# Linear attention and two MLPs in float32: w3 and w_out folded in plain float32, weights converted in pairs, the attention's diagonal by TensorE

## The chip, the cores and the metric

One core of one Trainium2 chip runs the whole kernel in one launch. The metric is device time in microseconds, the median of several executions. PE is the matmul engine (TensorE), DVE is VectorE, ACT is ScalarE, POOL is GpSimd, and SP is the engine whose queue issues the DMAs.

## The reference

```python
# r, k, v, w: (4, 8, 768, 48); u: (8, 48)
for t in range(S):
    cur = einsum('bhd,bhe->bhde', u[None] * kt, vt)
    y[:, :, t] = einsum('bhd,bhde->bhe', rt, state + cur)
    state = wt[:, :, :, None] * state + einsum('bhd,bhe->bhde', kt, vt)
x = y.transpose(0, 2, 1, 3).reshape(3072, 384)
x = (((x @ w1) * (x @ w2)) @ w3) @ w_out        # w1, w2 384x1024, w3 1024x1024, w_out 1024x384
h = x @ w_in                                     # 384x2048
return (h - tanh(h)) @ w_out2                    # 2048x384
```

r, k, v, w and u are float32. The weights of the two MLPs are 64-bit floats, which the kernel receives as pairs of 32-bit words and turns into float32 itself.

## The kernel before

**Weights.** `conv` (L123) loads a block of 64-bit words by a DMA on SP's queue into tile st (four buffers of 384 columns), and makes the float32 bits in tile cm: ScalarE takes the absolute value with a scale (L130), VectorE a minimum (L131), ScalarE the three low bits (L135, or VectorE in L138 and L139 for the second MLP), VectorE shifts and joins them (L136) and puts the sign in (L140). ScalarE then copies a rounded first half (fp32r, L142) and GpSimd subtracts it for the second half (L143). A product of two such tensors is `three`: three fp32r matmuls, first by second, first by first, second by first half (L155 to L157).

**Fold.** w3 @ w_out has no activation between, so the kernel multiplies them once into a 1024 x 384 matrix W. WJ cuts its eight row blocks into groups of 2, 3 and 3; each group runs over the eight blocks m of the inner dimension, converts a piece of w3 (`fold`, L305), and sums in PSUM; `fold_end` (L315) splits the sums into halves. w_out is converted along the first group.

**Attention.** The 768 steps of each batch are cut into chunks of 128; 24 chunks in all. `prep(n)` (L184) loads one, scans the decays (L207, L214), inverts block ends (R, L210 and L211), scales k and r, and sums r, u and k over a head for the diagonal cd (L218 to L221). `att(n)` (L224) multiplies k by r (psA), copies, masks by GpSimd (L242) and sets the diagonal (from chunk PED = 5 on by VectorE, L247; before that by a scaled v and an identity matmul, L287), updates the state Sb (psk, psu, L262 to L271), and sums state and masked products into psy, which becomes block n // 4 of the first MLP's input. PSUM has five banks for `big` tiles (psa, psb, acc, psW, some psh) and three for `att` tiles.

**Blocks.** The 3072 tokens are six blocks of 512. `moe1` makes for each of eight f the products psa and psb (`phase1`, L333), their product g on VectorE, and, LA1 = 2 steps later, the product with W into acc (`phase2`). Along each block the four chunks of the next block's attention are issued. w1 and w2 are converted before and during block 0; 4 of the 32 pieces of the second MLP's weights in blocks 1 to 4, 16 in block 5 and the rest in the first block of `moe2`, which runs the second MLP over six blocks.

The order of the code is the priority of the work; a planner with a table of costs puts each engine's instructions in order ahead of time, and each engine then runs its list strictly in that order. All DMAs of the kernel stand in SP's one queue. A slower path behind a flag (L544 on) is not taken with these inputs.

Of the kernel before, what the change touches and what calls it, by code (L numbers as in the profile page):

```python
# [19 lines left out]
NP = H // 2  # L20
# [54 lines left out]
def body(ctx: ExitStack, tc, rT, kT, wP, wS, vN, rN, kN, vT, u, uP, w1, w2, w3T, wo, win, wo2, out):  # L75
# [6 lines left out]
    wtp = pool("wt", 28)  # L82
# [17 lines left out]
    ub = const.tile([128, DM], F32, name="ub")  # L100
# [22 lines left out]
    def conv(src, dst, n, by_act=True):  # L123
        st = cvp.tile([128, n, 2], I32, tag="st", name="st", bufs=4)
        nc.sync.dma_start(st.rearrange("p a b -> p (a b)"), src.bitcast(I32))
        lw, hw = st[:, :, 0], st[:, :, 1]
        lb = st.rearrange("p a b -> p (a b)").bitcast(U8)[:, 3::8]
# [17 lines left out]
    def wtile(name):
        return wtp.tile([128, 2, 384], F32R, tag="wt", name=name)

    def conv_w(src, name, p=None, by_act=True):
        t = p.tile([128, 2, 384], F32R, tag="wt2", name=name) if p else wtile(name)
        conv(src, t, 384, by_act)  # L150
        return t
# [13 lines left out]
    Sb = [a1.tile([128, NP, 128], F32, name=f"Sb{i}") for i in range(2)]  # L165
# [18 lines left out]
    def prep(n):  # L184
# [5 lines left out]
        r_n = a1.tile([128, DM], F32, tag="rn", name="rn")  # L190
        k_n = a1.tile([128, DM], F32, tag="kn", name="kn")
# [5 lines left out]
        nc.sync.dma_start(r_n, rN[n])  # L197
        if n == 0:
            nc.sync.dma_start(ub, u.to_broadcast([128, DM]))
        nc.sync.dma_start(k_n, kN[n])  # L200
# [9 lines left out]
        nc.vector.tensor_scalar(out=R, in0=P[:, :, SB::SB], scalar1=1e-25, scalar2=None, op0=ALU.max)  # L210
# [4 lines left out]
        (nc.vector if n < KD else nc.gpsimd).tensor_mul(fl(k_d), fl(k_d), sx)  # L215
        nc.gpsimd.tensor_mul(r_d, r_d, P[:, :, 0:C])

        nc.gpsimd.tensor_mul(r_n, r_n, ub)  # L218
        nc.gpsimd.tensor_mul(r_n, r_n, k_n)
        cd = a2.tile([128, H], F32, tag="cd", name="cd")  # L220
        nc.vector.tensor_reduce(out=cd, in_=r_n.rearrange("p (h d) -> p h d", d=D), op=ALU.add, axis=AX.X)  # L221
        preps[n] = r_d, k_d, P, v_n, cd

    def att(n):  # L224
# [27 lines left out]
        if c < NC - 1:  # L252
# [6 lines left out]
            for h in range(H):  # L259
                p, q = divmod(h, 2)  # L260
                o = 64 * q
                nc.tensor.matmul(pu[o : o + D, p, :], ks[:, p, o : o + D], v_n[:, h, :D], start=True, stop=True)  # L262
            for q in range(2):
                o = 64 * q
                dst = Sn[o : o + D, :, o : o + D]
                pt = P[o : o + D, :, C : C + 1].to_broadcast([D, NP, D])
                if c == 0:
                    nc.vector.tensor_mul(dst, pu[o : o + D], pt)
                else:
                    nc.vector.tensor_add(dst, pu[o : o + D], So[o : o + D, :, o : o + D])  # L270
                    nc.gpsimd.tensor_mul(dst, dst, pt)  # L271
# [5 lines left out]
        for p in range(NP if c else 0):  # L277
            nc.tensor.matmul(py[:, p, :], So[:112, p, :], r_d[:112, p, :], start=(p == 0), stop=False, skip_group_check=True)
# [24 lines left out]
    w1t, w2t, Wt = [None] * NF, [None] * NF, [None] * NF  # L303

    def fold(acc, m, j, wot):  # L305
        n = WJ[j + 1] - WJ[j]
        t = gp.tile([128, 2, 384], F32R, tag="g", name="w3")
        conv(w3T[m][:, WJ[j] * 128 : WJ[j + 1] * 128], t[:, :, : n * 128], n * 128)
        for i in range(n):
            three(  # L310
                acc[i][:, :DM], lambda h: t[:, h, i * 128 : (i + 1) * 128], lambda h: wot[m][:, h, :],
                m == 0, m == NF - 1,
            )

    def fold_end(acc, j):  # L315
        for i, a in enumerate(acc):
            w = wtile("W")
            nc.scalar.copy(w[:, 0, :], a[:, :DM])
            nc.vector.tensor_sub(w[:, 1, :], a[:, :DM], w[:, 0, :].bitcast(F32))
            Wt[WJ[j] + i] = w  # L320

    def fold_acc(j):
        return [big.tile([128, TB], F32, tag="big", name="psW") for _ in range(WJ[j + 1] - WJ[j])]

# [342 lines left out]
```

## Time and profile before

| | |
|---|---|
| median of 3 runs | 952.38 us (950.01 to 952.45) |
| profiled execution | 952.03 us, span 950.1 us, granted PE clock 0.962 |
| busy in the span | PE 877.3 us, DVE 703.6, ACT 497.6, POOL 290.2 |
| chain that ended last | PE 61%, DVE 22%, issue 6%, DMA 5%, POOL 3% |

The span reaches from the first to the last instruction. Busy time is the union of an engine's instructions; matmuls are pipelined, so a record's length is not its cost: the distance between two starts is. An idle time is shown with what ended it.

### The profile page before, as it was taken

Reading aid. Unit: us, or ns where it says so; the run is one execution under the profiler, and the core shown is the slowest. Engines: PE = TensorE matmul, PEld = TensorE weight load, DVE = VectorE, ACT = ScalarE, POOL = GpSimd, SP = SyncE. Lnnn points to the kernel's source line nnn. Section 1 sums busy time; section 2 is a strip of 40 time slices with the busy share of each in tenths; the row PEclk is TensorE's granted clock in tenths of the full one; section 3 lists DMA queues with packets and bytes.
Section 4 is the critical chain, followed back from the end, with each engine's and each line's share of the span. In section 5 each row is a group of like instructions: output and inputs, shape, how many; then the busy total and the mean of one; then the engine's idle time right before and its main releaser. Section 6 shows DMA issues by size and latency. Waiting matters only on the chain.

```text
span 950.1 us, 13117 instructions
## 1 busy us (share of the span) xinstructions
PE 877.3 (92%) x4626; PEld 710.2 (75%) x4626; DVE 703.6 (74%) x1101; ACT 497.6 (52%) x927; POOL 290.2 (31%) x283
## 2 busy tenths in 40 slices
PE   3678969889999999998999989999999999999997
PEld 2467657667778777776887768888888888888885
DVE  7999999986656657656369998677676666676764
ACT  5565656533333323333245676566676576665663
POOL 5786756534434334334124512010010010000000
PEclk9777979999999999997999999999999999999999
DMA  8656745454344234333025420020020010200001
GB/s 290 200 195 188 240 156 174 142 164 136 117 115 140 95 97 152 113 94 93 1 69 186 145 78 22 1 67 1 1 67 0 26 42 1 67 1 1 34 1 37
DMA packets 45434, 89.00 MB, mean 94 GB/s; under 512 B 5424, under 2 KB 11696, under 8 KB 45360
## 3 DMA queue, kind: packets, MB, share of 16 engines
q1 hardware_dynamic: 45360, 88.09, 29.9%
q8 instruction: 38, 0.62, 0.3%
q14 instruction: 36, 0.29, 0.1%
HBM read 76.27 MB, written 9.44 MB: 90 GB/s over the span
## 4 chain that ended last, share of the span: by engine, by line
PE 61%; DVE 22%; issue 6%; DMA 5%; POOL 3%; ACT 2%; SPq 0%; DVEq 0%; POOLq 0%; ACTq 0%
PE acc L157 9%; PE acc L155 9%; PE acc L156 9%; PE psh L155 7%; PE psh L156 7%; PE psh L157 7%; DVE cm L140 3%; DVE cm L131 3%; DVE cm L136 2%; DVE P L207 2%; PE psb L155 2%; PE psa L155 2%; DVE A L247 2%; PE psb L157 2%; PE psb L156 2%
## 5 line engine op out<-in xcount | busy, mean ns | idle before, releaser
L155 PE MATMUL psh<-xt,w 128*128 128x512 f32 x288 | 112.5, 391 | 0.5 <-DVE g L331 0.5
L156 PE MATMUL psh<-xt,w 128*128 128x512 f32 x288 | 112.3, 390 | 0.0
L157 PE MATMUL psh<-xt,w 128*128 128x512 f32 x288 | 112.2, 390 | 0.0
L156 PE MATMUL acc<-g,w 128*128 128x512 f32 x288 | 112.0, 389 | 0.0
L157 PE MATMUL acc<-g,w 128*128 128x512 f32 x288 | 111.9, 389 | 0.0
L155 PE MATMUL acc<-g,w 128*128 128x512 f32 x288 | 111.3, 389 | 0.0
L143 POOL TENSOR_TENSOR w<-cm,w 128x384 fp32r<-128x384 f32 (+1 forms) x72 | 81.5, 1138 | 87.0 <-ACT w L142 85.1
L327 POOL TENSOR_TENSOR xt<-x2l,xt 128x512 fp32r<-128x512 f32 x18 | 24.0, 1350 | 249.2 <-ACT xt L326 247.5
L390 DVE TENSOR_TENSOR psh<-psh,z 128x512 f32<-128x512 f32 (+1 forms) x99 | 67.4, 681 | 42.8 <-ACT z L387 42.0
L331 DVE TENSOR_TENSOR g<-psh,g 128x512 fp32r<-128x512 f32 (+1 forms) x99 | 66.5, 672 | 42.4 <-ACT g L330 41.9
L387 ACT ACTIVATE z<-psh 128x512 f32<-128x512 f32 (+1 forms) x99 | 57.9, 584 | 71.3 <-PE psh L157 69.7
L330 ACT CAST g<-psh 128x512 fp32r<-128x512 f32 (+1 forms) x99 | 56.7, 574 | 57.4 <-DVE psh L392 56.0
L330 ACT CAST g<-psb 128x512 fp32r<-128x512 f32 x48 | 28.0, 586 | 95.1 <-DVE psb L344 95.0
L155 PE MATMUL psb<-xt,w 128*128 128x512 f32 x144 | 61.5, 427 | 16.4 <-DVE g L331 9.2
L392 DVE SCALAR_TENSOR_TENSOR psh<-s,psh 128x512 f32<-128x512 f32 (+1 forms) x99 | 67.1, 678 | 8.7
L391 DVE SCALAR_TENSOR_TENSOR psh<-s,psh 128x512 f32<-128x512 f32 (+1 forms) x99 | 67.1, 678 | 8.5 <-ACT s L388 0.5
L388 ACT ACTIVATE s<-z,qa 128x512 f32<-128x512 f32 (+1 forms) x99 | 70.5, 712 | 2.7
L389 ACT ACTIVATE s<-z,qa 128x512 f32<-128x512 f32 (+1 forms) x99 | 68.9, 695 | 0.0
L142 ACT CAST w<-cm 128x384 fp32r<-128x384 f32 (+1 forms) x72 | 36.0, 502 | 56.4 <-DVE cm L140 52.4
L155 PEld LDWEIGHTS psh<-xt,w 128*128 128x128 f32 x288 | 54.3, 188 | 12.9 <-DVE g L331 1.6
L156 PEld LDWEIGHTS psh<-xt,w 128*128 128x128 f32 x288 | 54.2, 188 | 11.2
L157 PEld LDWEIGHTS psh<-xt,w 128*128 128x128 f32 x288 | 54.2, 188 | 11.2
(112 smaller groups left out, 2126.0 us busy)
## 6 DMA issues: line engine op xcount, KB each, us to landing
st<-wo SPq DMA_DIRECT2D x24, 384.0 KB, 3.2
P<-wP SPq DMA_DIRECT2D x24, 258.0 KB, 3.5
ws<-wS SPq DMA_DIRECT2D x24, 256.0 KB, 2.9
kd<-kT SPq DMA_DIRECT2D x24, 256.0 KB, 3.2
rd<-rT SPq DMA_DIRECT2D x24, 256.0 KB, 3.3
vn<-vN SPq DMA_DIRECT2D x24, 256.0 KB, 3.6
st<-w3T SPq DMA_DIRECT2D x16, 384.0 KB, 4.1
st<-w SPq DMA_DIRECT2D x16, 384.0 KB, 3.3
```

Source lines behind the costliest of these rows:

```text
L143: nc.gpsimd.tensor_sub(dst[:, 1, :], t, dst[:, 0, :].bitcast(F32))
L155: nc.tensor.matmul(ps, lhs(0), rhs(1), start=start, stop=False)
L156: nc.tensor.matmul(ps, lhs(0), rhs(0), start=False, stop=False)
L157: nc.tensor.matmul(ps, lhs(1), rhs(0), start=False, stop=stop)
L330: nc.scalar.copy(t[:, 0, :], x)
L331: nc.vector.tensor_sub(t[:, 1, :], x, t[:, 0, :].bitcast(F32))
L387: nc.scalar.activation(out=z, in_=p, func=AF.Square)
L388: nc.scalar.activation(out=s1, in_=z, func=AF.Square, scale=QS, bias=qa[:, 0:1])
L389: nc.scalar.activation(out=s2, in_=z, func=AF.Square, scale=QS, bias=qa[:, 1:2])
L390: nc.vector.tensor_mul(p, p, z)
L391: nc.vector.scalar_tensor_tensor(out=p, in0=s1, scalar=QB1, in1=p, op0=ALU.add, op1=ALU.mult)
L392: nc.vector.scalar_tensor_tensor(out=p, in0=s2, scalar=QB2, in1=p, op0=ALU.add, op1=ALU.mult)
```

## The change

w3 and w_out are converted to float32 and multiplied as they are, one plain float32 matmul in place of three on halves. A conversion (`words`, for `conv`) covers up to 768 columns, and weights lie in pairs in memory: w1 with w2, w_in with w_out2, two blocks of w_out; tile st has two buffers. The halves of w1 and w2 are subtracted by VectorE, those of the second MLP's weights by GpSimd; all low bits go by ScalarE. Fold runs in groups of five and three, the first ahead of block 0, the second in its first three steps (LATE), with a lag of 3 there. Attention chunks are issued at steps 1, 3, 5, 7 of the first group, each with the next one's prep. The diagonal cd comes from r times k (`rk`) and four matmuls with u (psd), copied by ScalarE. R is computed by GpSimd. k and r are scaled by VectorE for the first KD = 4 chunks and by GpSimd after, rk likewise. The state tile has 64 columns for two heads' 48 in separate row halves, so its update is one instruction where there were two, and its product with r eight matmuls of 48 rows where there were four of 112.

```diff
-WJ = 0, 2, 5, 8
-FIRST = 5, 8, 10, 11
-CONV = 3
-EARLY = 20, 20, 22
-KD = 6
+WJ = 0, 5, 8
+SLOTS = 14
+FIRST = 1, 3, 5, 7
+CONV = 2
+LATE = 3, 3, 2
+KD = 4
...
+    def words(src, n, dst=None):
+        st = cvp.tile([128, n, 2], I32, tag="st", name="st", bufs=2)
+        nc.sync.dma_start(fl(st), src.bitcast(I32))
...
+        to = m if dst is None else dst.bitcast(I32)
+        nc.vector.scalar_tensor_tensor(out=to, in0=hw, scalar=SIGN, in1=m, op0=ALU.bitwise_and, op1=ALU.bitwise_or)
+        return to.bitcast(F32)
...
+    def halves_of(src, name, vec=True):
+        t = wtile(name)
+        x = words(src, 2 * DM)
+        nc.scalar.copy(t[:, 0, :], x)
+        (nc.vector if vec else nc.gpsimd).tensor_sub(t[:, 1, :], x, t[:, 0, :].bitcast(F32))
...
-        nc.sync.dma_start(r_n, rN[n])
-        nc.sync.dma_start(k_n, kN[n])
...
-        nc.vector.tensor_scalar(out=R, in0=P[:, :, SB::SB], scalar1=1e-25, scalar2=None, op0=ALU.max)
+        nc.gpsimd.tensor_scalar(out=R, in0=P[:, :, SB::SB], scalar1=3e38, scalar2=1e-25, op0=ALU.min, op1=ALU.max)
...
-        (nc.vector if n < KD else nc.gpsimd).tensor_mul(fl(k_d), fl(k_d), sx)
-        nc.gpsimd.tensor_mul(r_d, r_d, P[:, :, 0:C])
-        nc.gpsimd.tensor_mul(r_n, r_n, ub)
-        nc.gpsimd.tensor_mul(r_n, r_n, k_n)
+        by = nc.vector if n < KD else nc.gpsimd
+        rk = a1.tile([128, NP, C], F32, tag="rk", name="rk")
+        by.tensor_mul(rk, r_d, k_d)
+        by.tensor_mul(fl(k_d), fl(k_d), sx)
+        by.tensor_mul(r_d, r_d, P[:, :, 0:C])
+        pd = attp.tile([128, NP, 2], F32, tag="att", name="psd")
+        for p in range(NP):
+            nc.tensor.matmul(pd[:, p, :], rk[:, p, :], ub[:, p, :], start=True, stop=True)
-        nc.vector.tensor_reduce(out=cd, in_=r_n.rearrange("p (h d) -> p h d", d=D), op=ALU.add, axis=AX.X)
+        nc.scalar.copy(cd, fl(pd))
...
-            nc.tensor.matmul(py[:, p, :], So[:112, p, :], r_d[:112, p, :], start=(p == 0), stop=False, skip_group_check=True)
+            for q in range(2):
+                o = 64 * q
+                nc.tensor.matmul(
+                    py[o : o + 64, p, :], So[o : o + D, p, :], r_d[o : o + D, p, :],
...
-            three(
-                acc[i][:, :DM], lambda h: t[:, h, i * 128 : (i + 1) * 128], lambda h: wot[m][:, h, :],
+            nc.tensor.matmul(acc[i][:, :DM], t[:, i * 128 : (i + 1) * 128], wot[m], start=m == 0, stop=m == NF - 1)
...
+            for f in range(NF):
+                if f < len(LATE):
+                    extra[f].append(lambda ms=range(at, at + LATE[f]): fold_late(ms))
+                    at += LATE[f]
...
-        if 0 < blk < NB - 1:
+        if 0 < blk <= SLOTS - NF - NF // 2:
             extra[4].append(conv2)
...
-                extra[f] += [lambda f=f: conv2(wp2 if f < 4 else None), conv2]
+                extra[f] += [conv2] * (2 if f < 2 else 1)
-        moe1(xtile(blk), blk, extra)
+        moe1(xtile(blk), blk, extra, lag=3 if blk == 0 else LA1)
```

## Rows read from the trace of the kernel before

**Rows 1.** Busy us of PE, PEld, DVE, ACT, POOL by stretch; granted clock; DMA.

```profile
0.00:205.00 205.00, 152.46 (x932) 122.05 (x933) 193.14 (x295) 116.45 (x247) 129.91 (x128) 0.88 0.63 196
205.00:495.00 290.00, 283.34 (x1770) 225.55 (x1769) 177.28 (x269) 99.56 (x202) 109.85 (x114) 0.98 0.35 105
495.00:575.00 80.00, 73.00 (x302) 58.08 (x301) 79.69 (x149) 49.84 (x94) 31.94 (x27) 0.96 0.41 129
575.00:950.00 375.00, 368.48 (x1627) 304.47 (x1625) 253.48 (x391) 231.79 (x385) 18.46 (x15) 0.99 0.07 22
```

**Rows 2.** Timeline of PE: start us, us, line, out<-in, shapes, records.

```profile
109.42 0.34 PE L156 MATMUL psW<-wo,w 128*128 128x384 f32 x1
109.59 0.39 PE L155 MATMUL psa<-xt,w 128*128 128x512 f32 x1
...
204.69 0.50 PE L155 MATMUL psa<-xt,w 128*128 128x512 f32 x1
```

**Rows 3.** Busy time of instructions on tile cm alone (VectorE, ScalarE, GpSimd).

```profile
0.00:205.00 205.00, 120.42 (x172) 53.44 (x107) 60.94 (x52) 0.88 0.63 196
```

**Rows 4.** Groups by line, VectorE, 0:205: busy us, mean ns | idle before.

```profile
L140 DVE SCALAR_TENSOR_TENSOR cm<-st,cm 128x384 int32<-128x384 int32 x47 | 39.6, 844 | 0.5
...
L214 DVE TENSOR_TENSOR_SCAN ws<-ws,ends 128x512 f32<-128x512 f32 x9 | 13.7, 1526 | 0.1
...
L210 DVE TENSOR_SCALAR R<-P 128x64 f32<-128x64 f32 x9 | 8.3, 925 | 0.1
...
L221 DVE TENSOR_REDUCE cd<-rn 128x8 f32<-128x384 f32 x10 | 5.4, 541 | 0.0
```

**Rows 5.** Timeline of VectorE, 124.6 to 127.2 us.

```profile
124.64 1.21 DVE L214 TENSOR_TENSOR_SCAN ws<-ws,ends 128x512 f32<-128x512 f32 x1
125.76 0.53 DVE L140 SCALAR_TENSOR_TENSOR cm<-st,cm 128x384 int32<-128x384 int32 x1
126.21 0.68 DVE L215 TENSOR_TENSOR kd<-kd,ws 128x512 f32<-128x512 f32 x1
126.81 0.35 DVE L131 TENSOR_SCALAR cm<-cm 128x384 f32<-128x384 f32 x1
```

**Rows 6.** Groups by line, VectorE, 900 to 950 us.

```profile
L391 DVE SCALAR_TENSOR_TENSOR psh<-s,psh 128x512 f32<-128x512 f32 x6 | 4.2, 696 | 0.6
...
L391 DVE SCALAR_TENSOR_TENSOR psh<-s,psh 128x256 f32<-128x256 f32 x6 | 2.6, 429 | 0.6
```

**Rows 7.** Groups by line, GpSimd (POOL), 0 to 205 us.

```profile
L143 POOL TENSOR_TENSOR w<-cm,w 128x384 fp32r<-128x384 f32 x36 | 42.4, 1180 | 24.5 <-ACT w L142 24.4
...
L242 POOL TENSOR_SCALAR_AFFINE_SELECT A<-A 128x512 f32<-128x512 f32 x17 | 13.4, 805 | 6.0 <-ACT A L240 6.0
```

**Rows 8.** Timeline of PE, one attention chunk at full clock.

```profile
297.88 0.56 PE L262 MATMUL psu<-vn,ks 128*48 128x48 f32 x16
298.38 1.16 PE L278 MATMUL psy<-rd,Sb 112*128 112x128 f32 x8
299.47 1.09 PE L281 MATMUL psy<-A,vn 128*64 128x128 f32 x16
...
300.93 1.93 PE L236 MATMUL psA<-rd,kd 48*128 48x128 f32 x16
302.78 0.50 PE L155 MATMUL psa<-xt,w 128*128 128x512 f32 x1
303.12 0.39 PE L156 MATMUL psa<-xt,w 128*128 128x512 f32 x1
303.35 0.40 PE L157 MATMUL psa<-xt,w 128*128 128x512 f32 x1
```

**Rows 9.** Waits of PE, 495 to 575 us: us, times, longest.

```profile
PE psb L155 <- DVE g L331: 4.0, 2, 2.1
```

**Rows 10.** Waits of SP's queue, 0 to 205 us: us, times, longest.

```profile
SPq L125 <- DVE cm L140: 93.0, 46, 6.6
```

**Rows 11.** DMA issues on the page: KB each, median us to landing.

```profile
st<-w3T SPq DMA_DIRECT2D x16, 384.0 KB, 4.1
```

More of the change, by code (lines that the diff above doesn't have):

```diff
@@ L74, in body @@
 @with_exitstack
-def body(ctx: ExitStack, tc, rT, kT, wP, wS, vN, rN, kN, vT, u, uP, w1, w2, w3T, wo, win, wo2, out):
+def body(ctx: ExitStack, tc, rT, kT, wP, wS, vN, vT, uB, uP, w12, w3T, wo, w45, out):
     nc = tc.nc
@@ L163, in body @@
     a2 = apool("a2", 2)
-    Sb = [a1.tile([128, NP, 128], F32, name=f"Sb{i}") for i in range(2)]
+    Sb = [a1.tile([128, NP, 64], F32, name=f"Sb{i}") for i in range(2)]
     for i in range(2):
@@ L261, in att @@
                 o = 64 * q
[L262 to L271, printed above, removed]
+                nc.tensor.matmul(pu[o : o + 64, p, :], ks[:, p, o : o + 64], v_n[:, h, :D], start=True, stop=True)
+            dst = Sn[:, :, :D]
+            pt = P[:, :, C : C + 1].to_broadcast([128, NP, D])
+            if c == 0:
+                nc.vector.tensor_mul(dst, pu, pt)
+            else:
+                nc.vector.tensor_add(dst, pu, So[:, :, :D])
+                nc.gpsimd.tensor_mul(dst, dst, pt)
         if n < PED:
@@ L451, in body, with conv2, fold_late @@
     per = TB // C
-    wot = []
     def conv1(f):
-        w1t[f] = conv_w(w1[f], f"w1_{f}")
-        w2t[f] = conv_w(w2[f], f"w2_{f}")
-    at = 0
-    for j in range(len(WJ) - 1):
-        acc = fold_acc(j)
-        for m in range(NF):
-            if j == 0:
-                wot.append(conv_w(wo[m], f"wo{m}"))
-            fold(acc, m, j, wot)
-            for n in range(per):
-                if FIRST[n] == at:
-                    att(n)
-            for f in range(CONV):
-                if EARLY[f] == at:
-                    conv1(f)
-            at += 1
-        fold_end(acc, j)
-    second = [(t, w, f) for f in range(NF2) for t, w in ((wint, win), (wo2t, wo2))][::-1]
-    def conv2(p=None):
-        if second:
-            t, w, f = second.pop()
-            t[f] = conv_w(w[f], f"w{f}", p, False)
-            if t is wint:
-                nc.vector.tensor_reduce(
-                    out=wm[:, :, f : f + 1], in_=t[f][:, 0, :].bitcast(F32).rearrange("p (a b) -> p a b", b=128),
-                    op=ALU.max, axis=AX.X, apply_absolute_value=True,
-                )
-    prep(per)
+        w12t[f] = halves_of(w12[f], f"w12_{f}")
+    second = list(range(NF2))[::-1]
+    def conv2(bound=True):
+        if not second:
+            return
+        f = second.pop()
+        w45t[f] = halves_of(w45[f], f"w45_{f}", False)
+        if bound:
+            nc.vector.tensor_reduce(
+                out=wm[:, :, f : f + 1], in_=w45t[f][:, 0, :DM].bitcast(F32).rearrange("p (a b) -> p a b", b=128),
+                op=ALU.max, axis=AX.X, apply_absolute_value=True,
+            )
+    prep(0)
+    acc = fold_acc(0)
+    for m in range(NF):
+        if m % 2 == 0:
+            conv_wo(m)
+        fold(acc, m, 0, wot)
+        for n in range(per):
+            if FIRST[n] == m:
+                att(n)
+                prep(n + 1)
+        if m >= NF - CONV:
+            conv1(m - NF + CONV)
+    fold_end(acc, 0)
+    late = []
+    def fold_late(ms):
+        if not late:
+            late.extend(fold_acc(1))
+        for m in ms:
+            fold(late, m, 1, wot)
+        if ms[-1] == NF - 1:
+            fold_end(late, 1)
     nxt = []
@@ L589, in body @@
                                 nc.sync.dma_start(xg[64 * q + D : 64 * q + 64, j, b, :], yo[a : a + 16])
-        wot = [conv_w(wo[m], "wo") for m in range(NF)]
+        wot.clear()
+        wo4.clear()
+        for m in range(0, NF, 2):
+            conv_wo(m)
         for j in range(len(WJ) - 1):
@@ L601, in body @@
                 drain(0)
+            spare.extend(sw.tile([128, 2, 2 * DM], F32R, name=f"spare{i}") for i in range(NF2 - SLOTS))
+            second.extend(range(NF2)[::-1])
             for f in range(NF2):
-                wint[f] = conv_w(win[f], "win", wp2 if f < 4 else None)
-                wo2t[f] = conv_w(wo2[f], "wo2")
+                conv2(False)
             with tc.For_i(0, NB, 1) as blk:
```

99 lines of the change are left out of this document (46 added, 53 removed).

## The prediction

> **What bounds the kernel now.** I read the busy time by stretch first, because the mean over the span hides three regimes [rows 1]. Up to 205 us VectorE is busy 193.1 of 205.0 us and PE 152.5, at a granted clock of 0.88. From 205 to 495 us PE is busy 283.3 of 290. From 495 to 575 us VectorE is busy 79.7 of 80 us again and PE 73.0. From 575 us PE is busy 368.5 of 375 with VectorE at two thirds. The timeline of PE then dates the first regime: block 0 of moe1 starts its first matmul (psa) at 109.59 us, block 1 at 204.69 us [rows 2]. So the start of block 1 is the number to forecast, then what PE has to do after it, then the second VectorE stretch.
>
> What fills VectorE up to 205 us is conversion: instructions on tile cm hold it for 120.4 us [rows 3], and they are dearer than they need be: L140 at 384 columns takes 844 ns on average, and 0.53 us in a quiet moment; the scan L214 1526 ns against 1.21 us [rows 4, 5]. What runs beside them is GpSimd, 129.9 us up to 205 us, of which the subtractions L143 on w alone are 42.4 [rows 1, 7].
>
> **The change, part by part.** The sum is made against the profiled execution, 952.03 us with a span of 950.1; the median of the three runs, 952.38, is 0.04% above it.
>
> *VectorE up to the start of block 1.* A one-pass instruction takes 0.429 us at 256 columns and 0.696 at 512 [rows 6], so 0.16 us and 1.04 ns a column: 0.56, 0.83, 0.96 us at 384, 640, 768. L131 at 0.35 us for 384 [rows 5] I take as 0.16 us and half that slope: 0.49 and 0.55 us at 640 and 768. A call of words has one L131 and two one-pass instructions: 1.47, 2.15, 2.47 us. Up to block 1 there are 8 calls of 640 columns (fold in a group of five), 8 of 384 (group of three), 4 pairs of w_out and 8 pairs of w1 and w2 at 768: 17.2 + 11.8 + 29.6 = 58.6 us. The 8 subtractions of w1 and w2, now VectorE's, add 7.7. Neighbours overlap by some 0.05 us of 0.6 at their ends [rows 5], so about 0.92 of the 66.3 shows as busy: 61 us.
> By the same rates the 172 old instructions on cm would hold VectorE for 74 us; they hold it for 120.4, so 46 us are lost beside 129.9 us of GpSimd. GpSimd now loses the halves of w3, w_out, w1, w2 and the products with rn; it keeps the selects (13.4 us [rows 7]), the v and state products (half as many of the latter), gets R nine times (64 columns, taken as under the 0.8 us of a 512-column select) and three products for each of chunks 4 to 8, 15 x 1.2 us: 50 us or so. Scaled with it the conversions lose 18 us.
> The rest of VectorE was 193.1 - 120.4 = 72.7 us. R goes (8.3 us) and so does the reduction L221 (5.4 [rows 4]), six more products of 0.68 us come (rk, kd and rd for four chunks, 12 for 6), the state update becomes one instruction for two (some 2 us), and about 6 us of its contention go by the same scale: 55. Sum 61 + 18 + 55 = 134, and 140 with the 6 us before the first bytes have been worked on.
>
> The Trainium skill's page SBUF — State Buffer, section Who interferes with whom, calls the pair of ports that VectorE shares with GpSimd an exclusive lock: the later instruction blocks for the whole of the other. By that wording every microsecond of GpSimd could cost VectorE one; on cm the trace has 46 for 130. At one for one the new VectorE time would be 61 + 55 + 50 + 6 = 172 us, more than the PE sum below, and the forecast 2 us later.
>
> *PE up to the start of block 1.* Fold was 192 matmuls of 384 columns at 0.17 us [rows 2], 33 us. A plain float32 matmul appears as two records (16 for psA's 8 matmuls): 1.85 us for 16 records of 128 columns, 0.116 each, against 0.23 us for 512 columns of fp32r [rows 8]. No row has 384 plain columns. If columns set the 0.116, a matmul takes 2 x 3 x 0.116 = 0.69 us; if the weight load does, as little as two fp32r passes, 0.34. I take 0.65, near the first, since psu's 16 records of 48 columns take 0.50 us, so that time does follow columns: 64 x 0.65 = 41.6 us, bounds 22 and 44. Attention of eight chunks by rows 8: psu, psy's two parts and psA are 0.50 + 1.09 + 1.09 + 1.85, psk's four records 0.4: 4.9 us each, and 0.9 (another set like L281, in its shadow) for five of them: 43.7 us. The new psd has 8 records with 128 x 128 weights and 2 columns; there the weights set the time, which I put at psA's 0.116 a record, and a change between plain and fp32r costs 0.1 us (the first psa after psA takes 0.34 us, the next 0.23 [rows 8]): 1.0 us a chunk, 8 us. Block 0 up to block 1, 189 matmuls of 0.226: 42.7. Sum 136 us at full clock, 154 at the old stretch's 0.88, 164 with the 10 us before the first matmul. So PE would be the longer queue, with VectorE not far off, and two such queues don't mesh fully: VectorE alone at 193 ended at 205. I take 170 us in place of 204.7: **minus 35 us**. Floor: 146 (PE at full clock), minus 59. Ceiling: 195, by the staging of rival B, minus 10.
>
> *Blocks 1 to 4.* PE is the bound, so what VectorE or GpSimd saves there counts nothing; what is added to PE counts: psd 16 x 1.0 us, and the state update's 64 weight columns for 48, some 0.1 us x 13. The read of the state by 48-row halves has 16 records for 8; the halves sit in different rows and columns of the array, and psy's column halves already go two at a time (16 records in 1.09 us, as long as 8 full ones [rows 8]): 0, bounds 0 and +1.0 us a chunk. **Plus 17 us.** Least: PE idles 6.7 us in this stretch, which can swallow some, plus 9; most, with the halves one by one, plus 33.
>
> *Block 5.* VectorE, busy 79.7 of 80 us, gets 10 paired calls of three instructions for 20 single ones of four: 25 us, and contention, for some 45. ScalarE takes over the low bits, 10 passes of 768 columns, at most about 1 us each (VectorE's 0.96 the nearest), where it is busy 49.8 of 80 [rows 1]. VectorE falls to some 60 of 80, and the 7.0 us of PE idling (the longest waits are for g [rows 9]) mostly go: **minus 6 us**, bounds 0 and minus 10. In moe2's first block 4 paired calls replace up to 12 single ones under a full PE: 0.
>
> The loads of rN and kN go; those of weights carry the same bytes in half as many issues. Sum: 952 - 35 + 17 - 6 = **928 us**.
>
> **Rivals.**
> A, the first part meshes fully: block 1 starts at 146 us, 904 us in all. For it: the chain to a fold matmul loses its last two links, copy and subtract. Against: it needs PE at full clock, and the old stretch had 0.88.
> B, the staging ring holds. There were four buffers of 384 columns; now there are two of up to 768, and SP already waits 93 us for L140 to free them [rows 10]. A buffer is held for its landing (4.1 us at 384 KB for w3T [rows 11], so perhaps 5 at 768 KB) and for two ScalarE and three VectorE passes (5 us or more). At a hold of 10 to 13 us, half of it per call, 12 calls of 768 columns and 16 shorter ones worth 10.7 take 113 to 148 us, under 170. It decides from a hold of 15 us; at 17 block 1 starts at 195 and the time is 953. Behind the held st on SP's queue stand the loads of the next preparation.
> C, slower: psd waits in PE's queue. Its rk comes from VectorE for four chunks, then from GpSimd, where it stands among products of 1.2 us and selects of 0.8; all block matmuls are queued behind psd, and it takes one of three att banks until ScalarE has copied it. With w us in each of chunks 8 to 23 the time is 928 + 16 w: a loss from 1.5 us, 968 at 2.5. Against: rk needs two loads and no scan, so it can be ready early.
> D, the float32 fold at a low clock. At 0.72 in place of 0.88, PE's 136 us are 189, block 1 starts at 199 us, and the time is 957. Against: PE is used more densely than before.
>
> **How the numbers follow.** Forecast (912 to 945) 0.66, A 0.12, B 0.09, C 0.07, D 0.06. The time is the forecast's, 928. Half of A lies below 905; most of C and half of B and D lie above 949: 0.2 is left out by 905 to 949. A difference under 0.3%, 3 us, can't be told from none here. Slower are C but for a short wait (0.06), two thirds of D (0.04) and a quarter of B (0.02): 0.12. No change takes a third of B and the rest of C: 0.04. Faster: 0.84.
>
> **What would show it.** Right: psa of block 0 near 80 us and of block 1 near 170; L131 and L140 near their quiet lengths; fold matmuls 0.65 us apart at full clock; psd 1 us a chunk; no PE gaps in block 5; moe2 as before. Wrong: SP waiting for st with VectorE idle (B), PE waiting for rk or cd (C), a clock under 0.8 up to block 1 (D), fold matmuls at 0.35 us, or any engine busier in block 5 than before.

## The result, and the profile after

The changed kernel takes 958.76 us (median; 954.84 to 966.62) beside 952.87 us for the kernel before on the same chips (950.01 to 955.07): a ratio of 1.006, 95% interval 1.0037 to 1.0083. It is slower, by 0.6%, where 928 us were forecast. The profiled execution took 959.94 us, with a span of 958.2, 8.1 us longer than before.

Busy time by stretch of the changed kernel, columns as in [rows 1]:

```profile
0.00:205.00 205.00, 165.09 (x993) 122.06 (x994) 147.26 (x211) 105.47 (x181) 60.17 (x63) 0.87 0.58 184
205.00:495.00 290.00, 285.12 (x1942) 227.35 (x1942) 161.93 (x207) 94.66 (x204) 102.41 (x103) 1.00 0.26 78
495.00:575.00 80.00, 75.57 (x320) 61.67 (x319) 66.62 (x94) 53.20 (x78) 31.14 (x17) 0.96 0.37 120
575.00:950.00 375.00, 375.00 (x1657) 310.22 (x1656) 257.65 (x396) 237.19 (x393) 19.17 (x15) 1.00 0.07 22
```

Up to 205 us VectorE fell from 193.1 to 147.3 us and GpSimd from 129.9 to 60.2: the work left them as forecast, and VectorE now idles 58 us there. But the timeline of PE shows what became of that:

```profile
97.32 0.77 PE L156 MATMUL psa<-xt,w 128*128 128x512 f32 x1 [6.60 <-DMA xt<-y]
...
199.21 0.76 PE L156 MATMUL psa<-xt,w 128*128 128x512 f32 x1 [3.92 <-DMA xt<-y]
...
500.87 0.39 PE L156 MATMUL psa<-xt,w 128*128 128x512 f32 x1
```

Block 1 starts at 199.2 us; before it was 204.7 [rows 2], and 170 was forecast. Block 5 starts at 500.9; before, its first psa was at

```profile
488.37 0.39 PE L155 MATMUL psa<-xt,w 128*128 128x512 f32 x1
```

So the span divides into: block 1's start 5.5 us earlier (forecast 35), blocks 1 to 4 301.7 us in place of 283.7, plus 18.0 (forecast plus 17), block 5 up to moe2's second block 113.8 in place of 118.0, minus 4.2 (forecast minus 6). Together plus 8.3, and the span says plus 8.1. One term of three was wrong, by 30 us. Of these, 17 had been lost before block 0, which starts at 97.3 us where "near 80" was forecast.

The waits of PE up to 205 us in the changed kernel (us in all, times, longest) give its idle time there, 39.8 us:

```profile
PE psa L156 <- DMA xt<-y: 10.5, 2, 6.6
PE psd L220 <- DVE rk L215: 8.6, 1, 8.6
PE psu L263 <- ACT ks L258: 4.9, 2, 2.8
PE psW L313 <- DVE cm L138: 4.7, 1, 4.7
PE psk L256 <- DVE y L299: 4.1, 1, 4.1
PE psb L156 <- DVE g L343: 3.1, 2, 1.9
PE psA L237 <- DVE y L299: 2.7, 1, 2.7
```

The second row is the start, 8.6 us; the other 31.2 are spread over many waits, for VectorE, ScalarE and the DMAs, none above 10.5. No single late producer is seen, so the cause had to be found by taking things away.

What did change in kind is ScalarE's waiting for weights. Its waits up to 205 us, first the kernel before, then the changed one:

```profile
ACT cl L135 <- DMA st<-w: 6.9, 5, 2.2
...
ACT cm L130 <- DMA st<-wo: 3.6, 2, 1.8
...
ACT cl L135 <- DMA st<-w3T: 2.7, 3, 1.4
```

```profile
ACT cm L131 <- DMA st<-w: 18.1, 8, 5.0
ACT cm L131 <- DMA st<-w3T: 13.9, 10, 4.2
...
ACT cl L135 <- DMA st<-w: 11.2, 5, 4.5
ACT cm L131 <- DMA st<-wo: 7.7, 4, 3.3
...
ACT cl L135 <- DMA st<-w3T: 3.2, 2, 1.7
```

From 14.1 us (with a fourth row of 0.9) to 54.1. In ScalarE's list the copies of ks, A, cd and y stand behind these waits. SP waits for the staging buffers about as long as before (93.0 us in [rows 10]):

```profile
SPq L127 <- DVE cm L138: 76.2, 27, 12.4
```

The last step to block 0 can be followed in the chain of waits (start, us):

```profile
89.56 0.30 DVE y L299
...
89.88 0.74 SPq L304
...
91.93 5.25 DMA xt<-y
...
97.32 0.77 PE psa L156
```

### The profile page after: what moved, and what is told of

Read it like the earlier page. It is cut to its first block, busy times and chain, and to the rows that moved or that the text cites. A ratio compares the mean times of both kernels' runs of the same rounds, so it can differ in the third digit from the quotient of the medians.

```text
span 958.2 us, 13061 instructions
## 1 busy us (share of the span) xinstructions
PE 902.6 (94%) x4914; PEld 722.5 (75%) x4914; DVE 634.8 (66%) x907; ACT 491.1 (51%) x855; POOL 212.9 (22%) x197
## 4 chain that ended last, share of the span: by engine, by line
PE 62%; DVE 14%; DMA 11%; ACT 5%; issue 5%; POOL 2%; SPq 1%; ACTq 0%; DVEq 0%; POOLq 0%
PE acc L157 9%; PE acc L156 9%; PE acc L158 9%; PE psh L156 7%; PE psh L157 7%; PE psh L158 7%; DMA st<-w 4%; DMA P<-wP 2%; DVE cm L138 2%; DVE P L204 2%; DMA st<-w3T 2%; DVE cm L136 2%; PE psa L156 2%; PE psb L156 2%; PE psa L158 2%
## 5 line engine op out<-in xcount | busy, mean ns | idle before, releaser
L157 PE MATMUL acc<-g,w 128*128 128x512 f32 x252 | 98.0, 389 | 0.0
L156 PE MATMUL psh<-xt,w 128*128 128x512 f32 x252 | 98.0, 389 | 0.0
L157 PE MATMUL psh<-xt,w 128*128 128x512 f32 x252 | 98.0, 389 | 0.0
L158 PE MATMUL acc<-g,w 128*128 128x512 f32 x252 | 97.9, 389 | 0.0
L158 PE MATMUL psh<-xt,w 128*128 128x512 f32 x252 | 97.9, 389 | 0.0
L156 PE MATMUL acc<-g,w 128*128 128x512 f32 x252 | 97.3, 389 | 0.0
L156 PE MATMUL psa<-xt,w 128*128 128x512 f32 x144 | 60.4, 419 | 10.5 <-DMA xt<-y 10.5
L156 PE MATMUL psb<-xt,w 128*128 128x512 f32 x144 | 60.3, 418 | 7.7 <-DVE g L343 3.8
L204 DVE TENSOR_TENSOR_SCAN P<-P,e 128x516 f32<-128x516 f32 x24 | 33.4, 1392 | 49.0 <-ACT d L200 35.4
L131 ACT ACTIVATE cm<-st 128x768 f32<-128x768 f32 (+2 forms) x44 | 36.2, 826 | 50.8 <-DMA st<-w 19.3
L356 DVE TENSOR_TENSOR psb<-psb,a 128x512 f32<-128x512 f32 x48 | 33.1, 689 | 41.7 <-PE psb L158 35.4
L158 PE MATMUL psb<-xt,w 128*128 128x512 f32 x144 | 58.5, 406 | 0.0
```

The lines of the kernel that those rows point to most:

```text
L156: nc.tensor.matmul(ps, lhs(0), rhs(1), start=start, stop=False)
L157: nc.tensor.matmul(ps, lhs(0), rhs(0), start=False, stop=False)
L158: nc.tensor.matmul(ps, lhs(1), rhs(0), start=False, stop=stop)
L204: nc.vector.tensor_tensor_scan(out=fl(P), data0=fl(P), data1=fl(e0), initial=0.0, op0=ALU.mult, op1=ALU.add)
```

## The experiments

Each is compared with the kernel before by the ratio of their times (95% interval in brackets); the kernel before, run beside each, had medians of 952.9 to 954.6 us. All starts are from the timeline of PE of one profiled execution, and "PE work" is block 1's start less all of PE's idle time ahead of it. Executions of one kernel spread by up to 12 us, so a few us between two starts can be chance. Nor has PE always done the same by block 1's start: of block 0's matmuls with W, 0.23 us each, 54 are done in the changed kernel, 57 in the kernel before, 58 in e17, 61 in e14, 63 in e3, e5 and e10. Edits are to the changed kernel, for e8 to the kernel before; lines left out are marked by "...".

| kernel | median us | ratio | block 0 | block 1 | block 5 | idle, PE work up to block 1 |
|---|---|---|---|---|---|---|
| before | 952.87 | 1 | 109.6 | 204.7 | 488.4 | 52.3, 152.4 |
| after | 958.76 | 1.006 [1.0037, 1.0083] | 97.3 | 199.2 | 500.9 | 39.8, 159.5 |
| e1 three buffers | 949.04 | 0.993 [0.9902, 0.9958] | 92.6 | 188.4 | 489.2 | 31.0, 157.5 |
| e11 two, cl in place | 960.71 | 1.0072 [1.0047, 1.0098] | 96.0 | 196.1 | 497.8 | 34.5, 161.5 |
| e4 pieces of 384 | 957.21 | 1.0038 [1.0019, 1.0056] | 96.5 | 188.4 | 489.1 | 31.7, 156.7 |
| e2 xt by ScalarE's queue | 951.03 | 0.9979 [0.9951, 1.0008] | 96.8 | 197.5 | 488.4 | 30.7, 166.8 |
| e3 no psd | 942.54 | 0.9876 [0.9839, 0.9912] | 106.8 | 198.5 | 484.0 | 45.4, 153.1 |
| e5 e1 and e3 | 933.03 | 0.9785 [0.9749, 0.9821] | 101.9 | 194.4 | 476.3 | 42.3, 152.1 |
| e6 e5 and e2 | 934.84 | 0.9791 [0.9749, 0.9833] | 100.6 | 196.7 | 476.0 | 46.2, 150.5 |
| e7 e1, e2, three ws | 939.56 | 0.9852 [0.9809, 0.9894] | 95.4 | 187.1 | 481.7 | 33.4, 153.7 |
| e8 plain fold alone | 941.27 | 0.9863 [0.9825, 0.9901] | 93.3 | 189.8 | 476.8 | 40.5, 149.3 |
| e10 e3, six of 384 | 949.57 | 0.9951 [0.9933, 0.997] | 100.4 | 198.4 | 490.1 | 46.9, 151.5 |
| e9 loads out | 942.5 | 0.9899 [0.9842, 0.9957] | 97.0 | 183.5 | 483.4 | 29.5, 154.0 |
| e13 e9, and ScalarE's passes out | 935.96 | 0.9807 [0.9771, 0.9842] | 89.6 | 180.8 | 477.6 | 26.3, 154.6 |
| e14 e9, and two VectorE passes out | 915.38 | 0.9606 [0.9559, 0.9652] | 80.8 | 161.1 | 458.7 | 17.4, 143.7 |
| e12 e9, and all four out | 910.82 | 0.9545 [0.9529, 0.9561] | 80.6 | 160.6 | 460.0 | 13.7, 146.8 |
| e16 e5, subtractions on GpSimd | 947.03 | 0.9927 [0.9908, 0.9945] | 100.7 | 196.6 | 487.4 | 43.6, 153.0 |
| e17 e5, KD = 0 | 948.51 | 0.9937 [0.9916, 0.9957] | 102.4 | 197.1 | 487.1 | 52.8, 144.3 |

**e1, e11, e4: the staging ring.**

```diff
-        st = cvp.tile([128, n, 2], I32, tag="st", name="st", bufs=2)
+        st = cvp.tile([128, n, 2], I32, tag="st", name="st", bufs=3)
...
-        l = cvp.tile([128, n], I32, tag="cl", name="cl", bufs=2)
+        l = st[:, :, 0]
```

> The changed kernel with three staging buffers of up to 768 columns in place of two; the room comes from writing the low bits (cl) over the low words in st. Theory R (the two-buffer staging ring sets the pace up to block 1: ScalarE waits about 50 us for st landings there, and PE behind it): these waits fall below 25 us, block 1 starts at 175 to 185 us in place of 199, and the time is 935 to 945 us. Theory Q (the loads and moves that stand in SP's one queue, above all xt<-y ahead of blocks 0 and 1, set the pace, whatever the number of buffers): block 1 starts within 4 us of 199 and the time stays at 955 to 962. Theory P (the PE work added by psd and plain float32 is the whole loss): no change, 955 to 962, with PE's gaps merely moved.

Block 1 starts 10.8 us earlier and the time is 9.7 us lower. Both fall between the ranges of theory R and of the others: R had the place right and took it for too much. In the timeline of PE:

```profile
188.43 0.47 PE L156 MATMUL psa<-xt,w 128*128 128x512 f32 x1 [2.42 <-DMA xt<-y]
```

The room for the third buffer comes from writing the low bits in place, so e11 makes that second edit alone:

> A control for the third buffer: the changed kernel with the low bits in place over st and still two buffers. If the third buffer was what gave 10 us, this stays at 955 to 962 us with block 1 at 196 to 203. If writing the low bits in place (or the other order that the planner then makes) gave them, 946 to 952.

```profile
196.05 0.47 PE L156 MATMUL psa<-xt,w 128*128 128x512 f32 x1 [1.99 <-DMA xt<-y]
```

Its time is no lower than the changed kernel's, so the gain in time is the third buffer's. Of the 10.8 us in block 1's start, 3.2 come with this second edit alone and 7.6 with the buffer. ScalarE's waits for st fall to 41.7 us in e1 (15.9, 12.8, 8.8 and 4.2), not under the 25 of theory R, and stay at 53.2 in e11. e4 leaves the ring's bytes as they are but cuts each conversion into pieces of at most 384 columns, four buffers of them:

```diff
+        for a in range(0, n, 384):
...
+            st = cvp.tile([128, w, 2], I32, tag="st", name="st", bufs=4)
...
+            l = cvp.tile([128, w], I32, tag="cl", name="cl", bufs=4)
```

> The changed kernel with every conversion cut again into pieces of up to 384 columns (st four buffers of 384, the same bytes in flight; min, shift and sign once a piece), the pairs kept in memory. Theory R: a finer ring with the same bytes frees each piece after 7 us, not 9, block 1 starts at 185 to 195 us despite some 20 more VectorE instructions a stage, and the time is 944 to 954. Theory that the number of VectorE instructions counts: block 1 starts at 203 to 210 us and the time is 962 to 970.

In the profiled execution block 1 starts at 188.4, as in e1, yet the median is 8 us above e1's; that execution was the fastest of e4's, and the table's starts speak for it alone. Not conclusive. Since e1 added bytes as well as a buffer, no run here shows which of the two counts.

**e2: the loads of xt.** They stand behind st on SP's queue and end PE's two longest waits of the first part.

```diff
-                    nc.sync.dma_start(xt[b : b + 16, :, j, :].bitcast(F32), y3[a : a + 16].bitcast(F32))
+                    nc.scalar.dma_start(xt[b : b + 16, :, j, :].bitcast(F32), y3[a : a + 16].bitcast(F32))
```

> The changed kernel with the six moves xt<-y of each block issued on ScalarE's queue, not SP's. Theory Q: PE's waits for xt<-y (6.6 and 3.9 us ahead of psa) go, block 1 starts 8 to 12 us earlier and the time is 946 to 951 us. Theory R: the moves are late because ScalarE and SP are both held by the ring; ScalarE, which waits for st itself, issues them no earlier, block 1 starts within 4 us of 199, 954 to 962.

Block 1 moves by 1.7 us where theory Q had 8 to 12, though the time, 951.03, is at the edge of Q's range. The gain is in blocks 1 to 4, 290.9 us for 301.7, where the order of all lists is another. PE idles 2.3 us there for 4.9 and its granted clock is 1.00 for 0.99; some of the work also stands ahead of block 1 now, whose PE work is 166.8 us for 159.5. Why the order makes these differences is open. In e6, on top of e5, it brings nothing.

> The changed kernel with three staging buffers, the diagonal as it was, and xt<-y on ScalarE's queue. The move of xt<-y gave 7 us by itself (951.0 against 958.8), but most of it between blocks 1 and 5. If that gain was a shorter way for xt<-y past waiting loads, it adds: 923 to 929 us. If it was a luckier order of PE's work about psd, which is gone here, nothing is added: 930 to 935 us.

**e3: the diagonal as before** (sums over a head on GpSimd and VectorE, with the loads of rN and kN).

```diff
-        rk = a1.tile([128, NP, C], F32, tag="rk", name="rk")
-        by.tensor_mul(rk, r_d, k_d)
...
-            nc.tensor.matmul(pd[:, p, :], rk[:, p, :], ub[:, p, :], start=True, stop=True)
+        nc.gpsimd.tensor_mul(r_n, r_n, ub)
+        nc.gpsimd.tensor_mul(r_n, r_n, k_n)
...
-        nc.scalar.copy(cd, fl(pd))
+        nc.vector.tensor_reduce(out=cd, in_=r_n.rearrange("p (h d) -> p h d", d=D), op=ALU.add, axis=AX.X)
```

> The changed kernel with the diagonal as it was: r and k loaded by token, two products on GpSimd, a reduction on VectorE; no rk, no psd. Theory P: 1.0 us of PE goes from each of chunks 8 to 23, 16 us, and 8.6 us at the start where PE waited for rk: 934 to 944 us, with blocks 1 to 4 shorter by 14 to 17 us from block 1's start to block 5's end. If the psd time was hidden in PE's idle time anyway, blocks 1 to 4 shorten by less than 6 us and the time is 950 to 958. Theory R alone says nothing of blocks 1 to 4 and leaves block 1 near 199 us.

Blocks 1 to 4 take 285.5 us, 16.2 less, and the time falls by 16.2. In the changed kernel a psd in that stretch looks like this (timeline of PE):

```profile
215.91 1.05 PE L220 MATMUL psd<-ub,rk 128*128 128x2 f32 x8
216.82 0.48 PE L156 MATMUL psb<-xt,w 128*128 128x512 f32 x1
217.13 0.40 PE L157 MATMUL psb<-xt,w 128*128 128x512 f32 x1
217.37 0.39 PE L158 MATMUL psb<-xt,w 128*128 128x512 f32 x1
```

0.91 us to the next start, and that one takes 0.31 where the next takes 0.24: 1.0 us a chunk, as forecast. But only fifteen of the 24 psd lie in this stretch (120 records of PE; 72 lie ahead), which makes 15 us. The rest of the 16.2 is a balance: psA is busy 22.4 us there for 28.9 and 9 matmuls with W fewer fall there (2 us), while PE idles 9.9 us for 4.9. Up to block 1 psd's removal is worth 0.7 us, with these 9 matmuls done there. The 8.6 us at the start didn't go either: PE now waits 11.0 us for kd.

**e5, e7, e10: the best version, and two that were to be better.** e5 is e1's and e3's edits together.

> The changed kernel with three staging buffers (low bits in place) and the diagonal as it was. If the two losses add, the third buffer takes 10 us (949.0 against 958.8) and the diagonal 16 (942.5): 930 to 935 us, block 1 at 186 to 190 us, 284 to 287 us from block 1's start to block 5's. If the rN and kN loads, back in SP's queue, eat what the third buffer gives, block 1 stays near 198 and the time at 940 to 943.

933.03 us, below both kernels and the fastest here that computes the reference. As times the two gains, 9.7 and 16.2, add up (25.7). By place they don't: block 1 starts at 194.4 us where 186 to 190 were expected, and blocks 1 to 4 take 281.9 where 284 to 287 were, so a sum as exact as this is partly chance.

> The changed kernel, psd included, with three staging buffers, xt<-y on ScalarE's queue, and three buffers in place of two for the decay load ws, for which SP's queue waits 33 us up to 199 us while the weights' loads stand behind it. Theory Q: with the queue's head free, block 1 starts at 172 to 181 us and the time is 932 to 940. If the head of the queue costs nothing once the ring has three buffers, block 1 starts at 186 to 190 us and the time is 942 to 949.

Block 1 starts at 187.1 us, 1.3 before e1's. But the edit didn't free the head of the queue: up to 199 us SP waits 34.6 us ahead of ws loads and 17.5 ahead of kd loads, where e1 has 51.7 ahead of ws. So what a free head would bring was not tested. The time still falls into theory Q's range, by blocks 1 to 4 (294.6 us for e1's 300.7), as in e2.

> Three buffers' bytes as six of 384 columns, conversions in pieces of up to 384, low bits in place, the diagonal as it was: against 933.0 with three buffers of 768. If a finer ring of the same bytes still helps, 926 to 931 us and block 1 at 186 to 191. If the added VectorE instructions (some 25 before block 1, 0.3 us each) cost what it gives, 931 to 938 and block 1 at 192 to 198.

e10 missed: 16.5 us above e5. In its profiled execution, its slowest and 19.5 us above e5's, 4.0 lie in block 1's start, 9.8 in blocks 1 to 4 and the rest after. Its ring holds the same bytes as e5's; why it loses so much is open.

**e8: the float32 fold alone**, on the kernel before, with nothing else of the change.

```diff
...
-            three(
-                acc[i][:, :DM], lambda h: t[:, h, i * 128 : (i + 1) * 128], lambda h: wot[m][:, h, :],
-                m == 0, m == NF - 1,
+            nc.tensor.matmul(
+                acc[i][:, :DM], t[:, 0, i * 128 : (i + 1) * 128].bitcast(F32), wot[m][:, 0, :].bitcast(F32),
+                start=m == 0, stop=m == NF - 1,
```

> The kernel before with one part of the change alone: w3 and w_out stay plain float32 (no copy to the first half, no subtraction), one plain matmul in place of three; groups of 2, 3 and 3, single conversions and four staging buffers as before. If this part does what the prediction's sum said, some 37 us of GpSimd go before block 1, VectorE gets 13 of them back by the trace's share, PE takes 8 us more where it idles: block 1 starts at 188 to 196 us in place of 204.7 and the time is 937 to 945. If plain float32 on PE costs as much as it saves, block 1 stays at 202 to 207 and the time at 950 to 956.

Block 1 at 189.8, as expected: this part alone brings 14.9 us, more than the whole change's 5.5. The pairs with two buffers, and all that came with them (nine psd among it), gave 9.4 of it back.

**e9, e12, e13, e14: what holds block 1.** e9 loads one staging tile once for all conversions:

```diff
...
+        if not held:
+            held.append(cvp.tile([128, 2 * DM, 2], I32, tag="st", name="st", bufs=1))
+            nc.sync.dma_start(fl(held[0]), w12[0].bitcast(I32))
+        st = held[0][:, :n]
```

> The changed kernel with the weights' words loaded once: every conversion reads the same st tile, so there is no ring, no landing to wait for and no st load in SP's queue; the conversions' instructions are all there. It leaves out the loads of all weights but one (and scales them down), so its output is not the reference's. Theory R in full (all that the prediction missed up to block 1 is waiting for staged words): block 1 starts at 166 to 176 us, PE's gaps before it fall from 36 to under 20 us, and the time is 926 to 936. Theory S (the third buffer already took what staging costs, and the rest is the attention's chain between PE, ScalarE, GpSimd and VectorE ahead of blocks 0 and 1): block 1 starts at 183 to 190 us, with PE waiting for ks, y and xt<-y as before, and the time is 942 to 950.

> The kernel without loads of before (one st tile for all conversions), and each conversion cut to its last VectorE instruction, the sign; ScalarE's two passes and VectorE's other two are left out, so all weights are zero and the output is not the reference's. Copies, subtractions, fold, attention and blocks are there. The run without loads started block 1 at 183.5 us with some 21 us of PE's gaps behind the first 9. Theory S1 (PE's attention pieces wait for ScalarE and VectorE because conversions stand ahead of their copies in those engines' lists): PE's gaps after the start fall under 10 us and block 1 starts at 160 to 172 us. Theory S2 (the attention's own chain from PE to ScalarE, GpSimd, VectorE and back is as long whatever else is there): gaps stay at 16 to 24 us and block 1 starts at 176 to 184 us.

None of these four kernels computes the reference: e9's weights are all made from one block and scaled down, and those of the others are zero. The loads are worth 15.7 us of block 1's start, as theory S had it; five more than the third buffer. The conversions' first four passes are worth another 22.9. Which engine's? e13 takes ScalarE's two passes out of e9, e14 VectorE's first two; e12 has neither. Both e13 and e14 have zero weights, so what parts them isn't the data.

```diff
-        nc.scalar.activation(out=m.bitcast(F32), in_=hw.bitcast(F32), func=AF.Abs, scale=2.0**-113)
...
-        nc.scalar.activation(out=l, in_=fl(st).bitcast(U8)[:, 3::8], func=AF.Identity, scale=1 / 32, bias=qa[:, 5:6])
```

```diff
-        nc.vector.tensor_scalar(out=m.bitcast(F32), in0=m.bitcast(F32), scalar1=TOP, scalar2=None, op0=ALU.min)
...
-        nc.vector.scalar_tensor_tensor(out=m, in0=m, scalar=3, in1=l, op0=ALU.logical_shift_left, op1=ALU.bitwise_or)
```

> The kernel after with one staging tile loaded once for all conversions, and with the two ScalarE passes of each conversion left out; VectorE's three stay, at their sizes. The weights become zero, so the output is not the reference's. With the loads gone block 1 started at 183.5 us (942.5 us), and with two VectorE passes and both ScalarE passes gone as well at 160.6 (910.8). Theory C (ScalarE's list is what the conversions still hold up: its passes stand ahead of the copies ks, A, cd and y that PE waits for): block 1 at 160 to 167 us, 910 to 920 us in all. Theory D (VectorE's list is: three passes of each conversion ahead of kd, rk, A and y): block 1 at 176 to 184, 932 to 943. Theory L (the length of the whole chain ahead of a fold matmul, both engines' parts of it): half way, 168 to 175, 920 to 932.

> The kernel after with one staging tile loaded once for all conversions, and with VectorE's first two passes of each conversion left out; both ScalarE passes and VectorE's last pass stay. The weights become zero, so the output is not the reference's. Theory C (ScalarE's list is what holds PE up): block 1 at 176 to 184 us, 932 to 943 us in all. Theory D (VectorE's list is): block 1 at 160 to 167, 910 to 920. Theory L (the length of the chain through both): 168 to 175, 920 to 932.

Block 1's first psa in e9, then in e14:

```profile
183.50 0.39 PE L160 MATMUL psa<-xt,w 128*128 128x512 f32 x1
```

```profile
161.06 0.39 PE L158 MATMUL psa<-xt,w 128*128 128x512 f32 x1
```

The four busy-time rows, each up to its own block 1 start (e9, e13, e14, then e12 up to 160):

```profile
0.00:183.00 183.00, 153.52 (x978) 113.67 (x979) 143.34 (x208) 104.01 (x177) 59.80 (x63) 0.93 0.28 83
```

```profile
0.00:180.00 180.00, 153.72 (x979) 114.27 (x980) 144.78 (x209) 52.90 (x109) 59.69 (x63) 0.94 0.28 84
```

```profile
0.00:161.00 161.00, 143.49 (x981) 107.70 (x982) 103.47 (x144) 102.05 (x178) 53.14 (x63) 0.99 0.31 94
```

```profile
0.00:160.00 160.00, 146.20 (x972) 109.97 (x973) 105.98 (x143) 53.11 (x109) 57.40 (x63) 0.96 0.32 95
```

Half of ScalarE's time gone (104 to 53 us): block 1 moves 2.7 us. Forty of VectorE's 143 us gone: it moves 22.4, of which 12.1 are PE's idle time and 10.3 its work, at a granted clock of 0.99 in place of 0.93. e14's profiled execution was its fastest, 5.4 us below its median, so the 22.4 may be some us too many; 2.7 and 22.4 stay far apart. Theory D's ranges hold in both: VectorE's passes are what holds PE once the loads are gone, though VectorE is idle for 40 of e9's 183 us. Whether they do so by standing ahead of other work in its list or by their own length ahead of the fold's matmuls, these runs don't show.

**e16, e17: a lighter VectorE in a version that computes the reference.** Both are e5 with work moved to GpSimd, the eight subtractions for w1 and w2, or the scaling of k and r in the first four chunks.

```diff
-        w12t[f] = halves_of(w12[f], f"w12_{f}")
+        w12t[f] = halves_of(w12[f], f"w12_{f}", False)
```

```diff
-KD = 4
+KD = 0
```

> The version with three staging buffers and the diagonal as before (933.0 us, block 1 at 194.4), with the eight subtractions for the halves of w1 and w2 moved from VectorE (9.6 us busy) to GpSimd (2.2 us each, 18 us in all). Theory D (VectorE's list carries the time up to block 1): leaving out about 40 us of VectorE's passes brought 22 us, so 9.6 us bring about 5: block 1 at 188 to 191 us, 926 to 930 us in all. Rival P (GpSimd's 18 us beside it slow VectorE's other instructions by 0.4 us each, 7 us in all, and the second half is late by another 1.2 us): block 1 at 193 to 197, 931 to 937.

> The version with three staging buffers and the diagonal as before (933.0 us, block 1 at 194.4), with the scaling of k and r moved from VectorE to GpSimd for the first four chunks too (KD = 0): 6.3 us less on VectorE, 11 us more on GpSimd. Theory D: block 1 at 190 to 192 us, 928 to 931 us in all. Rival P (GpSimd's 11 us cost VectorE 4.5 us, and the scaled k and r, which the attention's first matmul waits for, come 1.3 us a chunk later): block 1 at 194 to 199, 932 to 939.

Theory D's sizes failed here, because VectorE's list didn't get lighter. Busy time up to 194 us in e5, e16 and e17:

```profile
0.00:194.00 194.00, 151.95 (x921) 108.29 (x921) 157.55 (x215) 102.71 (x170) 80.07 (x79) 0.92 0.68 222
```

```profile
0.00:194.00 194.00, 150.65 (x902) 106.86 (x903) 158.43 (x206) 103.14 (x169) 98.03 (x87) 0.90 0.68 221
```

```profile
0.00:194.00 194.00, 144.16 (x914) 102.56 (x914) 157.42 (x207) 102.93 (x170) 91.06 (x87) 0.91 0.67 221
```

9.6 us left VectorE in e16 and its busy time rose by 0.9: the rest of its work took 10.5 us more beside 18.0 us more of GpSimd. In e17, 6.3 left and 6.2 came back beside 11.0. The shift L136 at 768 columns, the same code in all three, took 1091 ns in e5, 1403 in e16 and 1277 in e17. Block 1 came 2.2 and 2.7 us later, as rival P had it; the times are 10 us above P's, and that excess lies in blocks 1 to 4 (290.8 and 290.0 us for 281.9), where the code is the same. By then e5 has done 9 matmuls with W more than e16 and 5 more than e17 (2.0 and 1.1 us), and in that stretch PE idles 12.3 and 9.5 us for e5's 7.8. What remains, and why the order of the lists does this, is open.

## Why the prediction was wrong, point by point

**The step that failed** is the one from two sums to a date: "PE would be the longer queue, with VectorE not far off, and two such queues don't mesh fully", for which 6 us were added to PE's 164. The sum itself was near: PE's work was 159.5 us where 154 were reckoned (198 block matmuls and nine psd for 189 and eight), and its start 8.6 for 10. The allowance was wrong: 31.2 us of idle time beyond the start. It was scaled on the kernel before, by VectorE's 193 us that ended at 205: a full engine's own slack. How long PE, the fed engine, idled in that same stretch (52.3 us, 42.4 of them after its start) stood in the trace and was not used.

What the runs put in the place of the 6: loads into two buffers, 10.8 us of block 1's start by a third buffer (7.6 against the control e11) and 15.7 without any loads; VectorE's first two passes, 22.4. With both out (e14) PE idles 9.0 us beyond its start, near the allowance, and block 1 starts at 161.1. PE's work times its granted clock is 140 us in the changed kernel and 142 in e14, where the sum had 136 at full clock: the sum holds. But e14's 161.1 also rests on a clock of 0.99. At the forecast's 0.88 its 143.7 us would be about 162 and block 1 would start near 179, an estimate by the ratio of the clocks. So 170 was early even for a kernel whose VectorE had 103 us of work and not 147.

**Rival B** had the place of the first loss and too low a price. It priced the ring as throughput, half a hold for each call, at 113 to 148 us for 28 calls, deciding from a hold of 15 us. A hold is the time from a load's issue to the last read of its buffer. Up to block 1 there were 33 of them, 360 us in all, 10.9 on average (the median is 10.2) and about 10 for the narrow pieces too: 180 us for each of the two buffers, 153 for the 28 calls. A full ring alone decides nothing: the four buffers before were held 785 us in 55 calls, as fully. What differs is that ScalarE, which waits in order for each landing, now waits 54.1 us for them in place of 14.1, and each late landing delays what stands behind it; the run without loads shows what the loads cost in all, 15.7 us.

**VectorE** was reckoned at 134 us busy and had 146.8. On cm it had 87.8 us, beside 60.2 of GpSimd (busy time of instructions on cm alone):

```profile
0.00:205.00 205.00, 48.64 (x128) 26.35 (x128) 87.76 (x107) 34.67 (x43) 3.75 (x2) 0.87 0.58 184
```

61 were reckoned for the quiet lengths of 28 calls and 18 for contention, by 46 us lost per 129.9 of GpSimd, 0.35 each. But 33 calls ran: five more of 768 columns, for the second MLP's weights, stand ahead of block 1, and the sum had left them out. Groups of VectorE up to 205 us:

```profile
L136 DVE SCALAR_TENSOR_TENSOR cm<-cm,cl 128x768 int32<-128x768 int32 x17 | 19.3, 1137 | 2.7 <-ACT cl L135 2.5
...
L136 DVE SCALAR_TENSOR_TENSOR cm<-cm,cl 128x640 int32<-128x640 int32 x8 | 7.0, 871 | 0.7 <-ACT cl L135 0.6
L136 DVE SCALAR_TENSOR_TENSOR cm<-cm,cl 128x384 int32<-128x384 int32 x8 | 5.8, 730 | 0.0
```

By the prediction's lengths these five are 12.4 us, 11 of them as busy time, nearly all that the 134 missed. So VectorE's conversions lost some 15 us by 60.2 of GpSimd, 0.26 each, where 18 were reckoned: the count of calls was wrong, not the contention. Whether the five calls delay block 1 no run shows. e16 and e17 give 0.58 and 0.56 for the work that they moved. The Trainium skill's SBUF — State Buffer, Who interferes with whom, calls this an exclusive lock; all these rates lie below the one for one that the prediction drew from that wording. That work moved from VectorE to GpSimd can be paid for on VectorE in full is what e16 and e17 show.

**Fold and psd** were priced well, each by itself. The timeline of PE in the first part:

```profile
46.06 1.05 PE L220 MATMUL psd<-ub,rk 128*128 128x2 f32 x8
46.97 3.47 PE L313 MATMUL psW<-wo,cm 128*128 128x384 f32 x10
50.38 0.71 PE L237 MATMUL psA<-rd,kd 48*128 48x128 f32 x4
```

Ten records in 3.41 us are five matmuls of 0.68 us (0.65 reckoned). So the float32 fold is 64 x 0.68 = 43.5 us of PE at full clock where it was 33 (busy up to 205 us, at the clocks granted, it was 48.6 us for 51.8), and it takes 1.4% off the time alone (e8), as VectorE, ScalarE and GpSimd lose the halves. The plus 17 for blocks 1 to 4 came as plus 18.0, in part by luck: there were fifteen psd for sixteen, the update cost its 1.4 us, and psA was busy 4.7 us longer than before (28.9 for 24.2), which the sum didn't have, while PE idled 1.8 us less.

**Rivals A, C and D.** A needed full clock and meshing; e14, without loads and with two VectorE passes less, comes to 161. C did not happen: beyond the start psd waits 0.2 us in all. D did not either: 0.87 up to 205 us where 0.88 was taken. Yet the clock is no fixed term: it was 0.93 in e9 and 0.99 in e14, where PE idled 12.1 us less. It doesn't go by the sum of PE's idle time alone: e12, with 13.7 us of it for e14's 17.4, had 0.96, and e17, with 52.8 for the changed kernel's 39.8, had 0.91.

**Block 5** was minus 4.2 for minus 6: PE's idle time there fell from 7.0 to 4.4 us, VectorE from 79.7 to 66.6 (60 reckoned).

## What to carry to other kernels

When work leaves the engine that fills a stretch, price the fed engine's date from its own idle time before, not from the busy sum of the next-longest engine: here 31 us of idling remained while no engine was over 81% busy. When the pieces of a staging ring grow and their number falls, look at which engine waits in order for the landings: a third buffer was worth 9.7 us here. Count the work that the planner brings forward into the stretch too (five calls here). Parts of a change are priced apart by where they act: the fold's gain was in the first part, psd's cost in every chunk after. Leaving psd out turns a loss of 0.6% into a gain of 1.2% (e3), and of 2.15% with the third buffer (e5).

## What had not been expected of the hardware

A matmul of two columns on 128 x 128 plain float32 weights costs what its weight loads do: psd's eight records take 0.91 us and their eight weight loads 0.97, and a record of 384 columns takes 0.34. Moving VectorE work to GpSimd moved no busy time off VectorE at all (157.6 us before, 158.4 and 157.4 after). And small edits that reorder every engine's list change blocks 1 to 4, with nearly the same work, by up to 10.8 us (e2 beside the changed kernel), as large as most effects sought here; the 22.4 us of e14 are twice that.
